# A decode step with grouped-query attention: the first softmax between two key halves, two small inputs as rows, the wait for the store in a section of its own

## The chip, the cores and the metric

The kernel runs on one core of one Trainium2 chip. The metric is the time of one execution on the device, in microseconds. A core has five engines that this kernel uses side by side: TensorE (PE: matrix products and transposes), VectorE (DVE), ScalarE (ACT), GpSimd (POOL, for a few fills at the start) and SyncE (SP, which here issues every transfer). Sixteen DMA engines carry the transfers. Engines run their own queues in order and wait for one another through semaphores.

## The reference, cut to what matters

One token `x` (512 values) goes through attention over a cache of 32,768 positions with 32 query heads on 8 key/value heads of width 128, and through a gated feed-forward layer; a gate computed from the token mixes the two.

```python
x = A_x                                             # (1, 1, 512)
g = sigmoid((x * gate_w).sum(-1, keepdims=True))
q = (x @ wq).reshape(B, Sq, 32, 128).transpose(0, 2, 1, 3)
k, v = repeat(k_cache, 4, axis=1), repeat(v_cache, 4, axis=1)   # caches: 1 x 8 x 32768 x 128
scores = einsum("bhqd,bhkd->bhqk", q, k) * 128 ** -0.5
o = einsum("bhqk,bhkd->bhqd", softmax(scores), v)
a = o.transpose(0, 2, 1, 3).reshape(B, Sq, 4096) @ wo
b = (silu(x @ w1) * (x @ w3)) @ w2                  # w1, w3: 512 x 1792
return g * a + (1 - g) * b
```

All is float32. The caches alone are 268 MB, and every byte is used once.

## The kernel before, in words

**Buffers.** Two large buffers in on-chip memory, `big_a` and `big_b`, have two halves of 4 MB each (32 KB on each of 128 partitions). Keys, values and the projection weights all pass through these halves.

**Start.** SP issues the two halves of `wq`, the token `x` and the gate weights between them, then `w1` and `w3` (L192 to L200). `x` and `gate_w` are laid out as 128 partitions by 4 values (`xs`, `gw`, L192 to L198). VectorE copies `xs` into the padded tile `xp` (L222), and TensorE multiplies `xp` with `wq` half by half (L250 to L261); the end of each half's products frees that half of `big_a` for keys. VectorE multiplies and adds `xs` and `gw` for the gate, TensorE sums over the partitions with a product with ones (L264 to L270). The feed-forward products follow (L290 to L309).

**The main loop.** The 8 key/value heads form four pairs, each pair is worked in four steps, and so there are 16 steps `t` (L444 to L463). A step has two halves of keys, `z` = 0 and 1, of 4 MB each. For one half, `scores` (L339) has VectorE turn the keys in 32 by 32 blocks, four instructions of 128 x 2048 into two buffers `kt` in turn, and TensorE multiply each quarter with a window of the queries (`winc`) that ScalarE copies ahead of the half (`window`, L325). After the two halves ScalarE copies the scores out (`scores_out`, L348) and TensorE clears its accumulator. `load_keys(t+1)` (L320) then puts the next step's two key loads into SP's queue. Each waits until TensorE has read the half that it overwrites. Keys go to `big_a`, only steps 1 and 3 go to `big_b`, before any values are there.

After every fourth step the pair's softmax is worked (`softmax(w)`, L364 to L397): TensorE turns the scores (four parts `f`, four transposes each), VectorE finds the maxima in 16 small and middling steps, subtracts them, ScalarE takes the exponentials, and VectorE sums these. In VectorE's queue all of it stands ahead of the next step's keys.

Values run some steps behind (`LAG` = 5, L142): from step 3 on, each step puts one 8 MB load of values into `big_b` (`load_values`, L400), behind the next step's two key loads. ScalarE copies the weights that belong to them (`weights`, L406), TensorE multiplies (`values_all`, L415), VectorE picks each head's own rows (`own`, L431).

**What sets the order.** The program lists the operations of all engines in one order by hand. A class `Program` (L24) records for each operation what it reads and writes, derives the semaphore waits and leaves out those that an earlier wait implies. Each engine's queue is then emitted in that order. Loads take one of 40 semaphores in turn (`load`, L182). TensorE's part of the main loop is a loop of its own on that engine (L658 to L673) that takes its permits from counting semaphores ("keys", "windows", "scores", "weights", "values"); its order is: values of an earlier step, windows and keys, clearing, and after each fourth step the four turning parts.

**End.** Output weights `wo` and the last values come through the same buffers, then `w2` (L554 to L634). VectorE copies the result out (L636), SP stores it (L637), waits for the store on SP (L643), and the section that holds the whole program (`tile_critical`, L151) closes when the function returns.

Of the kernel before, what the change touches and what calls it, by code (L numbers as in the profile page):

```python
# [9 lines left out]
ALU = mybir.AluOpType  # L10
AX = mybir.AxisListType
PE = mybir.EngineType.PE

P = 128
# [9 lines left out]
class Program:  # L24
# [16 lines left out]
            self.sems[name] = self.sem(name)  # L41
        return self.sems[name]

    def add(self, eng, fn, reads=(), writes=(), over=(), inc=None, by=1, credit=None, credits=(), loop=False):

        op = Op(eng, fn, credits, loop)
        clock = self.clock[eng]
        for c, _ in credits:
            for k, v in c.after.items():
                clock[k] = max(clock.get(k, 0), v)  # L50
        deps = {}
        for k in reads:
            assert k in self.writer, k
            deps[self.writer[k]] = True
        for k in (*writes, *over):
            if k in self.writer:
                deps[self.writer[k]] = True
            for r in self.readers.get(k, ()):
                deps.setdefault(r, False)
        need = {}  # L60
        taken = {c for c, _ in credits}
        for d, data in deps.items():
            if d in taken or (d.eng == eng and (eng == "PE" or not data)):
                continue
            if d.done is None:
                d = d.via
                if d is None or d.eng == eng:
                    assert d is not None
                    continue
            k, v = d.done  # L70
            if clock.get(k, 0) < v:
                need[k] = max(need.get(k, 0), v)
        for k, v in sorted(need.items(), key=lambda kv: -self.by[kv].index):
            if clock.get(k, 0) >= v:
                continue
            assert not loop, (fn, k, v)
            op.waits.append((k, v))
            for a, b in self.by[k, v].after.items():
                clock[a] = max(clock.get(a, 0), b)
        op.index = len(self.by)  # L80
        op.after = dict(clock)
        if credit:
            op.inc = (credit, by)
        elif inc is None and by == 0:
            op.inc = None
        else:
            s = inc or eng
            self.count[s] = self.count.get(s, 0) + by
            op.inc, op.done = (s, by), (s, self.count[s])
            op.after[s] = self.count[s]  # L90
            self.by[op.done] = op
        for c, _ in credits:
            c.via = op
        for k in reads:
            self.readers.setdefault(k, []).append(op)
        for k in writes:
            self.writer[k], self.readers[k] = op, []
        self.ops[eng].append(op)
        return op

# [14 lines left out]
def kernel(  # L115
# [32 lines left out]
    FJ = F // 4  # L148
    assert DH == P and D == 4 * P and REP == 4 and HKV == 8 and F == FR * P and S == 4 * P * NB

    ctx.enter_context(tc.tile_critical())  # L151
    pr = Program(nc, tc.alloc_semaphore)
    pe, dve, act, pool = (
        lambda fn, _e=e, **kw: pr.add(_e, fn, **kw) for e in ("PE", "DVE", "ACT", "POOL")
# [26 lines left out]

    def load(dst, src, writes, over=()):  # L182
        lanes[0] += 1
        return pr.add(
            "SP", lambda: nc.sync.dma_start(dst, src), writes=writes, over=over,  # L185
            inc=f"load{lanes[0] % 40}", by=16,
        )

    def region(b, z):
        return big[b][:, z * R:(z + 1) * R]  # L190

    xs, gw = sbuf("xs", NC), sbuf("gw", NC)  # L192
    wqd = wq.rearrange("(p c) n -> p (c n)", c=NC)
    for z in range(2):
        load(region(0, z), wqd[:, z * R:(z + 1) * R], [f"A{z}"])
        if z == 0:
            load(xs, x.rearrange("a b (p c) -> p (a b c)", p=P), ["xs"])
            load(gw, gate_w.rearrange("(p c) -> p c", p=P), ["gw"])  # L198
    for z, t in enumerate((w1, w3)):
        load(region(1, z)[:, 0:NC * F], t.rearrange("(p c) f -> p (c f)", c=NC), [f"B{z}"])  # L200

# [17 lines left out]
    dve(lambda: V.memset(xp, 0.0), writes=["xp0"])  # L219
    dve(lambda: V.memset(ones, 1.0), writes=["ones"])  # L220
    dve(lambda: V.memset(win, 0.0), writes=["win0"])
    dve(lambda: V.tensor_copy(xp[:, :, 0], xs), reads=["xs", "xp0"], writes=["xp"])  # L222

    for src, dst, view, axes in (
        ("ident", "fold", "p (c r) -> p r c", dict(c=4)),
# [21 lines left out]
    clear()  # L247


    for c in range(NC):  # L250
        def part(c=c):
            t = region(0, c // 2)
            for b in range(2):
                for j in range(4):
                    o = ((c % 2) * HKV + 4 * b + j) * REP * DH
                    ins = T.matmul(  # L256
                        pf[b][32 * j:32 * j + 32, :], xp[:, c, :], t[:, o:o + REP * DH],
                        start=(c == 0), stop=(c == NC - 1),
                    )
            return ins  # L260
        pe(part, reads=[f"A{c // 2}", "xp"], writes=["f0", "f1"])  # L261


    gpr, gsm = sbuf("gpr", NC), sbuf("gsm", 1)  # L264
    dve(lambda: V.tensor_mul(gpr, xs, gw), reads=["xs", "gw"], writes=["gpr"])
    dve(lambda: V.tensor_reduce(gsm, gpr, axis=AX.X, op=ALU.add), reads=["gpr"], writes=["gsm"])
    pe(lambda: T.matmul(pm[0][:, 0:1], ones, gsm, start=True, stop=True), reads=["ones", "gsm"], writes=["m0"])
    act(lambda: A.activation(gate[:, 0:1], pm[0][:, 0:1], AF.Sigmoid), reads=["m0"], writes=["gate0"])
    dve(lambda: V.tensor_scalar(gate[:, 1:2], gate[:, 0:1], -1.0, 1.0, op0=ALU.mult, op1=ALU.add),
        reads=["gate0"], writes=["gate1"])  # L270
# [87 lines left out]
    def turn_part(f):  # L358
        for a in range(4):
            ins = T.transpose(pf[f][:, P * a:P * a + P], sb[:, 4 * f + a].rearrange("p i m -> p (i m)"), ident)  # L360
        return ins

    def softmax(w):
        for f in range(4):  # L364
            pe(lambda f=f: turn_part(f), reads=[("sb", m) for m in range(4)] + ["ident"], writes=[f"f{f}"], loop=True)
            dve(lambda f=f: V.tensor_reduce(mx[:, f, :], pf[f].rearrange("p (n q) -> p q n", q=8), axis=AX.X, op=ALU.max),  # L366
                reads=[f"f{f}"], writes=[("mx", f)])

        dve(lambda: V.tensor_reduce(mt[:, 0:8], mx.rearrange("p f q -> p q f"), axis=AX.X, op=ALU.max),
            reads=[("mx", f) for f in range(4)], writes=["mt"])  # L370
        dve(lambda: V.transpose(mtt, mt), reads=["mt"], writes=["mtt"])
        for k in range(4):
            dve(lambda k=k: V.tensor_reduce(quads[0:32, k:k + 1], mtt[32 * k:32 * k + 32, :], axis=AX.X, op=ALU.max),  # L373
                reads=["mtt"], writes=[("quads", k)])
        dve(lambda: V.tensor_reduce(high[0:32, :], quads[0:32, :], axis=AX.X, op=ALU.max),
            reads=[("quads", k) for k in range(4)], writes=["high"])
        for k in range(4):
            dve(lambda k=k: V.tensor_copy(wide_t[32 * k:32 * k + 32, :], high[0:32, :].to_broadcast([32, 32])),  # L378
                reads=["high"], writes=[("wide_t", k)])
        dve(lambda: V.transpose(top, wide_t), reads=[("wide_t", k) for k in range(4)], writes=["top"])  # L380
        for f in range(4):
            d = rows[f % 2]
            dve(lambda f=f, d=d: V.tensor_tensor(  # L383
                d.rearrange("p (n q) -> p n q", q=8), pf[f].rearrange("p (n q) -> p n q", q=8),
                top[:, 0:8].unsqueeze(1).to_broadcast([P, 64, 8]), op=ALU.subtract,
            ), reads=[f"f{f}", "top"], writes=[f"row{f % 2}"])
            for u in range(2):
                act(lambda f=f, u=u, d=d: A.activation(  # L388
                    prob[u][:, 0:1024].rearrange("p (y n q) -> p n y q", y=16, q=4)[:, 4 * f:4 * f + 4],
                    d.rearrange("p (a y u q) -> p a y u q", a=4, y=16, u=2)[:, :, :, u],  # L390
                    AF.Exp, scale=SCALE,
                ), reads=[f"row{f % 2}"], writes=[("prob", u, f)])
        for u in range(2):
            dve(lambda u=u: V.tensor_reduce(  # L394
                sums[:, 8 * w + 4 * u:8 * w + 4 * u + 4], prob[u][:, 0:1024].rearrange("p (n q) -> p q n", q=4),
                axis=AX.X, op=ALU.add,
            ), reads=[("prob", u, f) for f in range(4)], writes=[("sums", w, u)])  # L397
# [46 lines left out]
    for t in range(NH):  # L444
        scores(t, 0, first)
        second = window(t, 1)
        if t >= LAG:
            own(t - LAG)
        if t >= LAG - 1:
            s = t - LAG + 1  # L450
            vals[s] = (vals[s], weights(s))
        scores(t, 1, second)
        scores_out(t)
        if t + 1 < NH:
            load_keys(t + 1)
        if t % 4 == 3:
            softmax(t // 4)
        if t + 1 < NH:
            first = window(t + 1, 0)
            if t >= LAG - 1:  # L460
                values_loop(*vals.pop(t - LAG + 1))
            if t >= LAG - 2:
                vals[t - LAG + 2] = load_values(t - LAG + 2)  # L463
# [176 lines left out]

    for e in ("SP", "ACT", "DVE", "POOL"):
        pr.emit(e)
    nc.sync.wait_ge(pr.semaphore("out"), 16)  # L643
    ops = pr.ops["PE"]
    a = next(i for i, o in enumerate(ops) if o.loop)
    b = max(i for i, o in enumerate(ops) if o.loop) + 1
# [11 lines left out]
    with nc.Fori(0, NP, 1, engines=[PE], head_slot={PE: 0}):  # L658
# [13 lines left out]
        for f in range(4):  # L672
            turn_part(f).then_inc(done, 1)  # L673
    pr.emit("PE", ops[b:])


# [26 lines left out]
```

## Time and profile before

| | us |
|---|---|
| median of 3 runs | 702.18 (701.09 to 702.6) |
| the profiled execution | 700.87 |
| its span in the profile | 699.1 |
| PE busy | 400.0 (57%) |
| DVE busy | 387.1 (55%) |
| ACT busy | 46.7 (7%) |
| key turning (L344, 128 instructions) | 285.9 of DVE's time |
| one key half, issue to landing, median | 28.1 |

The kernel moves 296.23 MB in the span, 424 GB/s. In the profile's views, an instruction's line is its line in the printed code; "idle before" is the time that the engine waited ahead of an instruction, with the engine or transfer that ended the wait. SPq is SP's queue: its entries are the issue of transfers, not the transfers. The DMA share of a stretch is the mean busy share of the 16 DMA engines; a packet is counted whole where the profile puts it, so the share of a short stretch can pass 1. PEclk is the share of TensorE's full clock that was granted.

### The profile page before, as it was taken

The numbers are of one execution on the slowest core, as the hardware profiler recorded it, in microseconds if no ns is written. First come the engines' busy times: TensorE is split into PE (matmuls) and PEld (weight loads), VectorE is DVE, ScalarE is ACT, GpSimd is POOL, SyncE is SP. The second block draws the span as 40 slices with busy tenths as digits, with TensorE's granted clock in tenths as the row PEclk, the third lists the DMA queues.
The fourth block names the chain that finished last, engine by engine and source line by source line (L and its number), as shares of the span: only waits on it lengthen the run. The fifth ranks groups of instructions, "written<-read, shape, count | busy, mean of one in ns | idle before, by whom it ended". The sixth has DMA issues, their size and how long they took to land. (4 is left out here: it accounts for less than half of the span.)

```text
span 699.1 us, 5711 instructions
## 1 busy us (share of the span) xinstructions
PE 400.0 (57%) x2384; PEld 91.3 (13%) x2384; DVE 387.1 (55%) x320; ACT 46.7 (7%) x106; POOL 1.5 (0%) x12
## 2 busy tenths in 40 slices
PE   3526665547565565757555655557466563835546
PEld 0100110101010111101010102101010102201112
DVE  1129998795709087754629097735538196532113
ACT  0100000110100002010100002000101002000000
POOL 0000000000000000000000000000000000000000
PEclk9976779769868878756677777868777886776669
DMA  8999999999999999999999999999999999999995
GB/s 360 433 435 433 435 426 437 452 396 409 452 412 439 427 457 411 433 433 441 446 407 437 431 454 409 439 426 452 420 427 439 424 457 406 423 448 420 419 417 235
DMA packets 10563, 296.37 MB, mean 424 GB/s; under 512 B 1332, under 2 KB 1336, under 8 KB 2488
## 3 DMA queue, kind: packets, MB, share of 16 engines
q1 hardware_dynamic: 10552, 296.23, 98.7%
q8 instruction: 6, 0.10, 0.1%
q14 instruction: 5, 0.04, 0.0%
HBM read 296.23 MB, written 0.00 MB: 424 GB/s over the span
## 5 line engine op out<-in xcount | busy, mean ns | idle before, releaser
L344 DVE STREAM_TRANSPOSE kt<-big_a 128x2048 f32<-128x2048 f32 x112 | 250.1, 2287 | 174.0 <-DMA big_a<-in_A_k_cache_dram 173.3
L333 PE MATMUL ps<-kt,winc 128*32 128x512 f32 x1024 | 191.4, 829 | 143.2 <-PEq L655 143.2
L421 PE MATMUL ps<-big_b,pv 128*32 128x512 f32 x768 | 109.2, 733 | 54.9 <-PEq L655 54.9
L333 PEld LDWEIGHTS ps<-kt,winc 128*32 128x32 f32 x1024 | 26.9, 124 | 303.1 <-issue 303.0
L421 PEld LDWEIGHTS ps<-big_b,pv 128*32 128x32 f32 x768 | 29.9, 131 | 132.8 <-issue 132.7
L344 DVE STREAM_TRANSPOSE kt<-big_b 128x2048 f32<-128x2048 f32 x16 | 35.8, 2288 | 3.3 <-DMA big_b<-in_A_k_cache_dram 3.0
L241 PE MATMUL ps<-acc 128*128 128x512 f32 x34 | 21.5, 718 | 21.8 <-PEq L655 20.2
L514 DVE SCALAR_TENSOR_TENSOR acc<-wo_t,own_rows,acc 128x512 f32<-128x512 f32 x24 | 18.0, 752 | 25.8 <-DMA wo_t<-in_A_wo_dram 25.0
L327 ACT COPY winc<-win 128x128 f32<-128x128 f32 x32 | 9.7, 303 | 330.0 <-PE ps L333 330.0
L530 PE MATMUL ps<-big_b,prob 128*32 128x512 f32 x128 | 18.9, 744 | 21.8 <-DMA big_b<-in_A_v_cache_dram 21.8
L350 ACT COPY sb<-ps 128x512 f32<-128x512 f32 x16 | 17.0, 1060 | 151.2 <-PE ps L333 151.2
L530 PE MATMUL ps<-big_a,prob 128*32 128x512 f32 x128 | 20.2, 797 | 5.3 <-DMA big_a<-in_A_v_cache_dram 5.3
L366 DVE TENSOR_REDUCE mx<-ps 128x8 f32<-128x512 f32 x16 | 9.9, 683 | 16.7 <-PE ps L360 16.7
L256 PE MATMUL ps<-big_a,xp 128*32 128x512 f32 x64 | 10.7, 827 | 14.8 <-DVE xp L222 10.0
L394 DVE TENSOR_REDUCE sums<-prob 128x4 f32<-128x1024 f32 x8 | 15.5, 1980 | 1.9 <-ACT prob L388 1.9
L296 PE MATMUL ps<-big_b,xp 128*32 128x448 f32 x64 | 7.8, 639 | 8.9 <-DMA big_b<-in_B_w_dram 8.9
L388 ACT ACTIVATE prob<-row 128x256 f32<-128x256 f32 x32 | 10.7, 404 | 29.3 <-DVE row L383 28.8
L503 PE MATMUL ps<-each,spot 128*128 128x64 f32 x6 | 2.1, 448 | 18.3 <-DVE each L500 18.3
L514 DVE SCALAR_TENSOR_TENSOR acc<-wo_t,on,acc 128x512 f32<-128x512 f32 x4 | 3.0, 752 | 16.4 <-DMA wo_t<-in_A_wo_dram 16.3
L437 DVE TENSOR_REDUCE red<-tmp 128x128 f32<-128x1024 f32 x6 | 11.5, 1915 | 0.2
L383 DVE TENSOR_TENSOR row<-ps,top 128x512 f32<-128x512 f32 x16 | 10.4, 689 | 0.9 <-ACT prob L388 0.8
L241 PEld LDWEIGHTS ps<-acc 128*128 128x128 f32 x34 | 5.7, 209 | 39.1 <-issue 37.5
(82 smaller groups left out, 100.1 us busy)
## 6 DMA issues: line engine op xcount, KB each, us to landing
big_a<-in_A_k_cache_dram SPq DMA_DIRECT2D x28, 4096.0 KB, 28.1
big_b<-in_A_k_cache_dram SPq DMA_DIRECT2D x4, 4096.0 KB, 31.4
big_a<-in_A_v_cache_dram SPq DMA_DIRECT2D x4, 4096.0 KB, 33.8
big_a<-in_A_wq_dram SPq DMA_DIRECT2D x2, 4096.0 KB, 16.7
wo_t<-in_A_wo_dram SPq DMA_DIRECT2D x4, 2048.0 KB, 18.1
big_b<-in_B_w_dram SPq DMA_DIRECT2D x2, 3584.0 KB, 33.6
big_b<-in_A_v_cache_dram SPq DMA_DIRECT2D x1, 4096.0 KB, 27.7
big_a<-in_B_w_dram SPq DMA_DIRECT2D x3, 1024.0 KB, 30.8
```

The source lines that it names most:

```text
L241: return T.matmul(ps_s, acc[:, 0:P], acc, start=True, stop=False, skip_group_check=True)
L256: ins = T.matmul(pf[b][32 * j:32 * j + 32, :], xp[:, c, :], t[:, o:o + REP * DH], start=(c == 0), stop=(c == NC - 1),)
L333: ins = T.matmul(ps_s[32 * g:32 * g + 32, :], winc[:, c, :], kt[c % 2][:, 512 * g:512 * g + 512], start=False, stop=False, skip_group_chec ...
L344: k = dve(lambda c=c, d=dst: V.transpose(d, kin[:, c]), reads=[key], writes=[f"kt{c % 2}"], credit="keys")
L350: lambda: A.copy(sb[:, :, :, t % 4], ps_s.rearrange("p (n i) -> p n i", i=32)),
L383: dve(lambda f=f, d=d: V.tensor_tensor(d.rearrange("p (n q) -> p n q", q=8), pf[f].rearrange("p (n q) -> p n q", q=8), top[:, 0:8].unsquee ...
L388: act(lambda f=f, u=u, d=d: A.activation(prob[u][:, 0:1024].rearrange("p (y n q) -> p n y q", y=16, q=4)[:, 4 * f:4 * f + 4], d.rearrange( ...
L394: dve(lambda u=u: V.tensor_reduce(sums[:, 8 * w + 4 * u:8 * w + 4 * u + 4], prob[u][:, 0:1024].rearrange("p (n q) -> p q n", q=4), axis=AX ...
L421: ins = T.matmul(ps_o[32 * t:32 * t + 32, :], pv[:, o:o + 32], big[1][:, n * P:(n + 4) * P], start=((z, g) == (0, 0)), stop=((z, g) == (1, ...
L437: dve(lambda: V.tensor_reduce(red[h], tmp.rearrange("p e b d -> p d (e b)"), axis=AX.X, op=ALU.add), reads=["tmp0", "tmp1"], writes=[("red ...
L514: dve(lambda k=k: V.scalar_tensor_tensor(acc, (wo_t if t is None else t)[:, k, :], o(k), acc, op0=ALU.mult, op1=ALU.add,), reads=[tkey, ke ...
L530: ins = T.matmul(ps_o[32 * t:32 * t + 32, :], prob[u][:, o:o + 32], vt[:, n * P:(n + 4) * P], start=((e, z, g) == (0, 0, 0)), stop=((e, z, ...
```

## The change

Four edits, in the order of the program:

1. Loads take one of 12 semaphores in turn instead of 40, and each load also depends on the load before it on the same semaphore (`lane`).
2. The token and the gate weights are loaded as one row of 512 values on one partition each, into the tiles `row0` and `row1`. TensorE turns the token's row into four columns (`columns`, four transposes) and VectorE copies these into `xp`, after its small set-up reductions. The gate's product and sum run over the 512 values on one partition, and the product with ones has one row.
3. TensorE's turning of the scores becomes a function of its own, `turn`, called where the softmax began. The rest of the first pair's softmax is called in step 4, after that step's first key half and ScalarE's copy for the second, ahead of the second half. The other pairs' softmaxes are called where they were, except that ScalarE's copy of the next window is listed ahead of them.
4. The section that holds the program closes before SP's wait for the store, and that wait stands in a second section of its own.

```diff
     def load(dst, src, writes, over=()):
         lanes[0] += 1
+        lane = f"load{lanes[0] % 12}"
         return pr.add(
-            "SP", lambda: nc.sync.dma_start(dst, src), writes=writes, over=over,
-            inc=f"load{lanes[0] % 40}", by=16,
+            "SP", lambda: nc.sync.dma_start(dst, src), writes=writes, over=[*over, lane], inc=lane, by=16, also=lane,
         )
...
         if z == 0:
-            load(xs, x.rearrange("a b (p c) -> p (a b c)", p=P), ["xs"])
-            load(gw, gate_w.rearrange("(p c) -> p c", p=P), ["gw"])
+            load(rows[0][0:1, :], x.rearrange("a b n -> (a b) n"), ["row0"])
+            load(rows[1][0:1, :], gate_w.rearrange("(o n) -> o n", o=1), ["row1"])
...
-    dve(lambda: V.tensor_copy(xp[:, :, 0], xs), reads=["xs", "xp0"], writes=["xp"])
...
+    def columns():
+        for c in range(NC):
+            ins = T.transpose(
+                pm[0][:, c:c + 1], rows[0][0:1, :].rearrange("o (p c) -> o c p", c=NC)[:, c, :], ident[0:1, 0:1]
+            )
+        return ins
+
+    pe(columns, reads=["row0", "ident"], writes=["m0"])
+    dve(lambda: V.tensor_copy(xp[:, :, 0], pm[0][:, 0:NC]), reads=["m0", "xp0"], writes=["xp"])
...
-    gpr, gsm = sbuf("gpr", NC), sbuf("gsm", 1)
-    dve(lambda: V.tensor_mul(gpr, xs, gw), reads=["xs", "gw"], writes=["gpr"])
-    dve(lambda: V.tensor_reduce(gsm, gpr, axis=AX.X, op=ALU.add), reads=["gpr"], writes=["gsm"])
-    pe(lambda: T.matmul(pm[0][:, 0:1], ones, gsm, start=True, stop=True), reads=["ones", "gsm"], writes=["m0"])
+    gpr, gsm = tmp[0:1, 1].rearrange("p b d -> p (b d)"), sbuf("gsm", 1)
+    dve(lambda: V.tensor_mul(gpr, rows[0][0:1, :], rows[1][0:1, :]), reads=["row0", "row1"], writes=["tmp1"])
+    dve(lambda: V.tensor_reduce(gsm[0:1, :], gpr, axis=AX.X, op=ALU.add), reads=["tmp1"], writes=["gsm"])
+    pe(lambda: T.matmul(pm[0][:, 0:1], ones[0:1, :], gsm[0:1, :], start=True, stop=True), reads=["ones", "gsm"], writes=["m0"])
...
+    def turn():
+        for f in range(4):
+            pe(lambda f=f: turn_part(f), reads=[("sb", m) for m in range(4)] + ["ident"], writes=[f"f{f}"], loop=True)
+
     def softmax(w):
         for f in range(4):
-            pe(lambda f=f: turn_part(f), reads=[("sb", m) for m in range(4)] + ["ident"], writes=[f"f{f}"], loop=True)
...
         scores(t, 0, first)
         second = window(t, 1)
+        if t == 4:
+            softmax(0)
         if t >= LAG:
             own(t - LAG)
...
         if t % 4 == 3:
+            turn()
+        if t + 1 < NH:
+            first = window(t + 1, 0)
+
+        if t in (7, 11, 15):
             softmax(t // 4)
         if t + 1 < NH:
-            first = window(t + 1, 0)
             if t >= LAG - 1:
...
-    nc.sync.wait_ge(pr.semaphore("out"), 16)
...
     pr.emit("PE", ops[b:])
+    critical.close()
+    with tc.tile_critical():
+        nc.sync.wait_ge(pr.semaphore("out"), 16)
```

In `Program.add`, `also` makes the operation the last writer of that name as well, and the first section is held in an `ExitStack` of its own so that it can be closed early.

More of the change, by code (lines that the diff above doesn't have):

```diff
@@ L42, in semaphore, with add @@
         return self.sems[name]
-    def add(self, eng, fn, reads=(), writes=(), over=(), inc=None, by=1, credit=None, credits=(), loop=False):
+    def add(self, eng, fn, reads=(), writes=(), over=(), inc=None, by=1, credit=None, credits=(), loop=False, also=None):
         op = Op(eng, fn, credits, loop)
@@ L97, in add @@
             self.writer[k], self.readers[k] = op, []
+        if also:
+            self.writer[also] = op
         self.ops[eng].append(op)
@@ L149 @@
     assert DH == P and D == 4 * P and REP == 4 and HKV == 8 and F == FR * P and S == 4 * P * NB
-    ctx.enter_context(tc.tile_critical())
+    critical = ctx.enter_context(ExitStack())
+    critical.enter_context(tc.tile_critical())
     pr = Program(nc, tc.alloc_semaphore)
@@ L190, in region @@
         return big[b][:, z * R:(z + 1) * R]
-    xs, gw = sbuf("xs", NC), sbuf("gw", NC)
     wqd = wq.rearrange("(p c) n -> p (c n)", c=NC)
```

## The prediction

> **What bounds the kernel.** I read the page's slices and DMA table first, then the stretches around the first softmax, then SP's and VectorE's instructions in order of time, and last the DMA packet records of the trace (start, length and bytes of each packet), transfer by transfer.
>
> ```profile
> DMA  8999999999999999999999999999999999999995
> q1 hardware_dynamic: 10552, 296.23, 98.7%
> ```
>
> SP's queue keeps the 16 DMA engines busy for 98.7% of the span, so only a hole in the DMA stream, or the two ends, can be worth anything. The packet records give the rate: a 32 KB packet takes 1.213 us, so a 4 MB transfer (eight packets on each engine) takes 9.71 us. From 208 to 586 us the last packets of the transfers come 9.68 to 9.72 us apart per 4 MB: no hole. One stretch breaks the pattern:
>
> ```profile
> core 0: us, PE busy (x) PEld busy (x) DVE busy (x) ACT busy (x) POOL busy (x), PEclk, DMA share, GB/s
> 140.00:150.00 10.00, 2.23 (x12) 0.46 (x16) 9.52 (x7) 1.66 (x6) 0.00 (x0) 0.50 0.98 426
> 150.00:160.00 10.00, 6.68 (x40) 0.79 (x32) 10.00 (x5) 0.82 (x2) 0.00 (x0) 0.82 0.90 370
> 160.00:170.00 10.00, 7.74 (x50) 1.82 (x54) 3.25 (x3) 1.16 (x2) 0.00 (x0) 0.83 0.94 400
> ```
>
> The DMA share falls to 0.90 while VectorE is busy for all of the 10 us. SP shows why (start, length of the group, line, count):
>
> ```profile
> 101.03 9.30 SPq L185 DMA_DIRECT2D big_a<-in_A_k_cache_dram  x2
> 130.22 0.33 SPq L404 DMA_DIRECT2D big_b<-in_A_v_cache_dram  x1
> 155.27 9.53 SPq L185 DMA_DIRECT2D big_a<-in_A_k_cache_dram  x2
> 173.84 0.33 SPq L404 DMA_DIRECT2D big_b<-in_A_v_cache_dram  x1
> ```
>
> I call the halves of step 5's keys k(5,0) and k(5,1), the value loads v(0), v(1). v(0) ends between 155.74 us (first engine) and 157.67 (last). k(5,0) is issued only at 155.27: it needs the buffer of k(4,0), which VectorE turns only after the first softmax:
>
> ```profile
> 119.46 8.95 DVE L344 STREAM_TRANSPOSE kt<-big_b 128x2048 f32<-128x2048 f32 x4 [1.14 <-DMA big_b<-in_A_k_cache_dram]
> 133.00 2.48 DVE L366 TENSOR_REDUCE mx<-ps 128x8 f32<-128x512 f32 x4 [4.58 <-PE ps L360]
> ...
> 145.06 17.73 DVE L344 STREAM_TRANSPOSE kt<-big_a 128x2048 f32<-128x2048 f32 x8
> ```
>
> VectorE waits 4.58 us for TensorE's transposes, then spends 133.00 to 145.06 on the softmax, while k(4,0), complete at 128.60, lies untouched. The first packet of k(5,0) starts 1.02 us after its issue, fifteen engines have begun by 157.68, the sixteenth begins at 158.81 (3.54 us after the issue). k(5,0) ends at 169.14, 11.47 us after v(0) instead of 9.71: **the hole costs the slowest engine 1.76 us**, and nothing later gives it back.
>
> **The change, part by part.**
>
> *1. The first softmax goes between the halves of step 4's keys.* Nothing is added; 12.06 us of VectorE work and the exps move behind four transposes. My rebuild, in the old run's times: k(4,0)'s last packet 128.60, plus the 0.57 us that k(3,1) took from its last packet (118.89) to the first transpose (119.46), gives 129.2. Two transposes of 2.24 (8.95/4) end at 133.6. The third overwrites a kt buffer that TensorE must have read; TensorE finishes its transposes at 134.3 and then takes 1.1 to 1.9 us for each of the four score groups (the clock granted decides). So the third starts at 135.4 to 136.2, the fourth ends at 139.8 to 140.7, and k(5,0) is issued at 141 to 142.7, over 12 us ahead of need: that hole is gone. Softmax: 140.3 + 12.06 = 152.3, four transposes to 161.3, TensorE's last group about 1.4 later: k(5,1) goes out near 162.7 (162.0 to 163.4; before, 164.47).
>
> What is late next is this k(5,1). Without the hole k(5,0) ends at 165.46 to 167.38. Fifteen engines get k(5,1) in time or are early ones with slack. The sixteenth would begin 3.5 to 4.2 us after the issue (k(5,0) and k(5,1) before), at 166.2 to 166.9, and a first packet after an idle engine is 0.35 to 0.65 longer: 177.2 at the end against 177.09 undisturbed; at the late end of the issue, 0.8 lost. I charge 0.25: **gain 1.5 us, bounds 0.8 and 1.76**. v(1) goes out some 9.4 us after k(5,1), as before, near 172.1, with k(5,1) ending at 175.2 or later: no new hole. SP issues in order and nothing overtakes. In the other pairs the window copy only moves ahead of the exps on ScalarE; VectorE's order and every release stay, and the queue there is 5.5 us or more ahead: nothing.
>
> *2. Token and gate weights as a row each.*
>
> ```profile
> xs<-in_A_x_dram SPq DMA_DIRECT2D x1, 2.0 KB, 11.9
> gw<-in_gate_w_dram SPq DMA_DIRECT2D x1, 2.0 KB, 12.0
> ```
>
> Each is 128 packets of 16 B now, 9 ns each: 16 data and 2 closing packets per engine, 0.16 us. The packets behind them are stretched by up to 0.37 us, and wq's second half ends at 22.34 to 23.30, where 9.71 after the first half's end (12.21 to 12.76) would be 21.92 to 22.47: lost 0.42 on the first engine, 0.83 on the last. A row is one piece of 2 KB; the closing store moves its four rows as one packet each, so I expect one packet on one engine, 88 ns as the 2,048-byte packets of wo take. Bounds of the gain: 0.83 if all goes, 0 if the stretching stays or falls on the slowest engine. I take **0.6**, nearer the upper end, as fifteen engines then have nothing to do.
>
> Added for it: four transposes on TensorE (0.27 us each, a pair every 0.2) and a copy of 0.17, some 1.0 us ahead of the first wq products (13.63 now). TensorE idles 4.74 us behind these before wq's second half lands, and the key load that they release (19.02) stands behind transfers that last until 40.9: hidden; uncovered it would cost 1.0. The gate's product and sum grow from 0.155 and 0.157 to about 0.69 and 0.68 (rows of 512 elements at L383 and L366), beside 14.36 us of VectorE waiting.
>
> *3. Twelve semaphores for loads.* A load also waits for the load twelve before it. At 28 us from issue to landing and 9.71 per load three or four are in flight; every wait is satisfied by the buffer's own: nothing.
>
> *4. The wait for the store in a section of its own.*
>
> ```profile
> L151 SPq NOP  x2: 17/18/18, 0.7 to 697.5; - x2
> L151 ACTq DRAIN  x1: 8/8/8, 697.2 to 697.2; - x1
> L698 SPq DRAIN  x3: 7/7/119, 697.6 to 698.4; - x3
> ```
>
> SP issues the store at 695.33 to 696.00 and passes its wait at 697.03. Only then do the section's closing steps run (L151, 697.19 to 697.52), then the program's (to 699.08). Now the first section closes beside the store's flight, and a second one, of SP alone, closes behind it. No engine has work queued behind. The gain is 0.33 if the second costs nothing; if it pays its own entry and close in full, 0.35 is lost. The clearing of semaphores (334 ns, on the chain) has 28 fewer to clear: 0 to 0.17. I take **0.25**, bounds 0.5 and -0.35.
>
> Sum: 1.5 + 0.6 + 0.25 = 2.35 us. The profiled execution took 700.87 us (span 699.1 and 1.77 around it), which becomes 698.5. The median shown, 702.18, lies 1.3 above it; the same saving there gives **699.8**.
>
> **A rule weighed.** The row first: a transfer that meets idle engines starts 1.02 us after its issue on the first and 3.54 on the last. The Trainium skill (DMA: Bandwidth & Descriptors, Specifications) gives a first-byte latency of about 0.6 us for loads issued from SP. By that, k(5,1) would start on every engine before it is due and part 1 would give 1.76. No packet of the trace began so soon after an issue, so the sum goes by the row.
>
> **The rivals.**
> - *A, the hole moves to k(5,1)* (chance 0.15). For: it is issued only 1.8 us earlier than before while its turn comes 1.76 us earlier. Against: 162.7 leaves the last engine about enough. If the issue stays at 164, part 1 gives 0.5: 702.18 - 0.5 - 0.85 = 700.8.
> - *B, slower: the softmax holds k(5,1) back* (0.07). It stands on VectorE ahead of the second half now; each us of issue past 163 costs one. The saving is eaten at 163 + 2.6 = 165.6. For: its exps bring a table load of 1.28 us, ScalarE's copy for the next window comes first, and TensorE's clock in this stretch was down to 0.50. Against: these lie beside 2.5 us of maxima and 2.5 us of small steps. At 167.5 it gives 702.18 + 1.9 = 704.1.
> - *C, only the softmax counts* (0.13): the rows stretch what follows as before and the second section costs 0.35: 702.18 - 1.5 + 0.35 = 701.0.
> - *D, every engine starts as early as the first did* (1.02 us after issue; 0.12), so k(5,1) loses nothing: 702.18 - 1.76 - 0.85 = 699.6. The Trainium skill's first-byte figure, above, points this way.
>
> The forecast has 0.53. **Chances**: the runs before differ by 1.5 us, so 0.2% (1.4 us) is about what a measurement of this kernel can tell from no change. Faster by more: forecast and D, 0.65; within: A and C, 0.28; slower: B, 0.07. **Range**: all bounds at their best save 1.76 + 0.83 + 0.5 = 3.1 (699.1), and the runs reach 1.1 below their median: 698.0. At the other end C and 1.3 for the spread of runs: 702.3. B and the tails are left out.
>
> **What would show it.** Right: keys of step 4 turned from 129 us, maxima after 139, k(5,0) issued at 141 to 143, k(5,1) at 162 to 163.5, the DMA share from 150 to 170 us near 1.0, packets under 512 B down from 1332 to about 1050, wq's second half landing 0.5 us or more sooner, L151's drains before the store's landing. Wrong: an issue of k(5,1) after 164, a last packet of step 5's keys less than 1 us before the old 178.89, or a chain behind the store longer than 2.05 us (697.03 to 699.08).

## The result and the profile after

| | before | changed |
|---|---|---|
| median of 5 runs | 701.15 us (701.07 to 702.6) | 698.40 us (698.34 to 698.44) |
| the profiled execution | 700.87 | 698.40 |
| its span | 699.1 | 696.5 |

The changed kernel takes 0.9954 of the time before (95% interval 0.994 to 0.9969): faster by 0.46%. Forecast were 699.8 us and 2.35 us saved; 698.4 us, and 2.75 us between these medians, came out. Where the runs before differ by 1.5 us, the five after lie within 0.1 us.

The page's DMA slices and table of the changed kernel, against a first slice of 8 and 98.7% before:

```profile
DMA  9999999999999999999999999999999999999995
DMA packets 10279, 296.37 MB, mean 426 GB/s; under 512 B 1046, under 2 KB 1050, under 8 KB 2204
q1 hardware_dynamic: 10268, 296.23, 98.9%
```

The bytes are the same, and 286 packets under 512 B are gone (1332 before): 256 of 16 B and 30 closing ones. SP's issues in order of time (start, length of the group):

```profile
100.41 10.38 SPq L189 DMA_DIRECT2D big_a<-in_A_k_cache_dram  x2
129.08 0.33 SPq L419 DMA_DIRECT2D big_b<-in_A_v_cache_dram  x1
139.98 22.02 SPq L189 DMA_DIRECT2D big_a<-in_A_k_cache_dram  x2
171.04 0.33 SPq L419 DMA_DIRECT2D big_b<-in_A_v_cache_dram  x1
```

k(5,0) goes out at 139.98 instead of 155.27. The group ends at 162.00 and one issue takes 0.33, so k(5,1) goes out at 161.67. This is a swap: one load goes out 15 us earlier, and the next, whose buffer now waits for the softmax, only 2.8 us earlier. VectorE in the same stretch:

```profile
118.86 8.96 DVE L356 STREAM_TRANSPOSE kt<-big_b 128x2048 f32<-128x2048 f32 x4 [0.51 <-DMA big_b<-in_A_k_cache_dram]
128.50 4.50 DVE L356 STREAM_TRANSPOSE kt<-big_a 128x2048 f32<-128x2048 f32 x2 [0.69 <-DMA big_a<-in_A_k_cache_dram]
134.21 4.50 DVE L356 STREAM_TRANSPOSE kt<-big_a 128x2048 f32<-128x2048 f32 x2 [1.21 <-PE ps L345]
138.64 2.44 DVE L381 TENSOR_REDUCE mx<-ps 128x8 f32<-128x512 f32 x4
...
150.68 8.94 DVE L356 STREAM_TRANSPOSE kt<-big_a 128x2048 f32<-128x2048 f32 x4
```

The wait of 4.58 us for TensorE's turning is now filled with two key transposes; 1.21 us of it is left ahead of the third. The softmax takes 12.04 us, 12.06 before.

In the packet records the last packet of k(5,0) comes 9.71 us after v(0)'s (11.47 before), that of k(5,1) 9.72 later: no hole. The 10-us shares show it less clearly:

```profile
150.00:160.00 10.00, 6.04 (x28) 0.92 (x32) 9.62 (x5) 0.00 (x0) 0.00 (x0) 0.50 0.95 410
160.00:170.00 10.00, 8.73 (x70) 2.20 (x66) 2.72 (x2) 1.17 (x2) 0.00 (x0) 0.93 1.01 433
```

The DMA shares (next to last column) are 0.95 and 1.01, where they were 0.90 and 0.94 before. Counted by the packets' own starts and lengths, the engines of the changed kernel are never idle from 150 to 170 us, and 0.95 us on average before. So 0.95 in a 10-us window is no hole here: 64 KB packets of 2.4 us fall to one window or the other.

The start and the end:

```profile
13.00 0.61 PE L253 MATMUL ps<-ident,row 1*128 1x1 f32 x4 [9.40 <-DMA row<-in_A_x_dram]
13.64 0.17 DVE L259 COPY xp<-ps 128x4 f32<-128x4 f32 x1 [10.01 <-PE ps L253]
13.72 0.67 DVE L277 TENSOR_TENSOR tmp<-row 1x512 f32<-1x512 f32 x1
```

```profile
L721 POOLq EVENT_SEMAPHORE_RANGE_CLEAR  x1: 182/182/182, 696.0 to 696.0; - x1
```

Four transposes and a copy put the first wq products at 13.86 (13.63 before). Each row moved as one packet of 2,048 B, 84 ns. wq's second half ends at 21.77 to 22.33, 0.97 us sooner on the last engine. From the store's issue to the end of the span 3.38 us pass (3.75 before); the clearing of semaphores fell from 334 to 182 ns.

### The profile page after: what moved, and what is told of

The parts are those of the page before. It is cut to its first block, busy times and chain, and to the rows that moved or that the text cites. A ratio compares the mean times of both kernels' runs of the same rounds, so it can differ in the third digit from the quotient of the medians.

```text
span 696.5 us, 5727 instructions
## 1 busy us (share of the span) xinstructions
PE 407.6 (59%) x2388; PEld 91.7 (13%) x2388; DVE 388.6 (56%) x320; ACT 46.5 (7%) x106; POOL 1.5 (0%) x12
## 5 line engine op out<-in xcount | busy, mean ns | idle before, releaser
L345 PE MATMUL ps<-kt,winc 128*32 128x512 f32 x1024 | 197.7, 854 | 134.4 <-PEq L675 134.3
L308 PE MATMUL ps<-big_b,xp 128*32 128x448 f32 x64 | 10.2, 803 | 9.5 <-DMA big_b<-in_B_w_dram 9.5
L268 PE MATMUL ps<-big_a,xp 128*32 128x512 f32 x64 | 9.3, 735 | 3.5 <-DMA big_a<-in_A_wq_dram 3.2
```

The source lines that it names most:

```text
L308: ins = T.matmul(pf[2 + z][32 * j:32 * j + 32, 0:FJ], xp[:, c, :], t[:, o:o + FJ], start=(c == 0), stop=(c == NC - 1),)
L345: ins = T.matmul(ps_s[32 * g:32 * g + 32, :], winc[:, c, :], kt[c % 2][:, 512 * g:512 * g + 512], start=False, stop=False, skip_group_chec ...
```

## The experiments

I went in with the theory of the prediction, now with the larger price: the hole behind v(0) is the main term, the start and the end are small. Rivals: the start and the end carry it, or the hole moves. The experiments were timed in three groups (e1 to e4, e5 to e8, e9 to e12), each on a chip of its own beside fresh runs of the kernel before.

### One part at a time

**e1**, the softmax moved and nothing else (`turn`, `softmax(0)` in step 4, the window copy ahead, on the kernel before; the copy's move was not tried alone):

```diff
+        if t == 4:
+            softmax(0)
...
         if t % 4 == 3:
+            turn()
+        if t + 1 < NH:
+            first = window(t + 1, 0)
+
+        if t in (7, 11, 15):
             softmax(t // 4)
         if t + 1 < NH:
-            first = window(t + 1, 0)
```

> The kernel before with the first softmax moved between the key halves of step 4, and nothing else. My theory (the hole behind v(0) cost the slowest DMA engine 1.76 us and nothing takes its place): 1.7 to 1.9 us less than before, k(5,0) issued near 140.6, k(5,1) near 162.3, the last packet of k(5,1) 19.4 us behind that of v(0). Rival 1 (the hole is only part; start and end made most of the 2.75 us): at most 1.2 us less. Rival 2 (the hole's cost varies from run to run and makes the spread of the runs before, 701.07 to 702.6): the runs of this kernel lie within 0.3 us of one another; if the spread has another source it stays near 1.5 us.

Measured: 699.10 us against 700.97 for the kernel before in this group, 1.87 less, ratio 0.9971 (0.9955 to 0.9986, or 1.0 to 3.2 us). Eleven of the twelve runs lie between 698.96 and 699.21, one at 700.3. SP's issues:

```profile
142.39 20.44 SPq L185 DMA_DIRECT2D big_a<-in_A_k_cache_dram  x2
171.88 0.33 SPq L407 DMA_DIRECT2D big_b<-in_A_v_cache_dram  x1
```

k(5,0) was issued at 142.39, k(5,1) at 162.51, and the last packet of k(5,1) came 19.42 us behind v(0)'s: no hole. The theory holds, and the runs are steady as rival 2 asked. Rival 1's 1.2 us is outside the median, though not clear of the interval; that the start and the end are small is shown by e5 to e8.

**e2**, the rows and nothing else (the diff's part 2 on the kernel before).

> The kernel before with token and gate weights as rows, and nothing else. My theory (the 256 packets of 16 B stretch what follows; rows are one packet each on one engine): wq's second half ends 0.6 to 1.0 us sooner, and 0.6 to 1.0 us off the whole. Rival (the hole behind v(0) takes it back, since k(5,0)'s issue follows the first softmax, and with it the landings, at the same distance): the hole moves along with the landings, so the gain stays; if instead the issue of k(5,0) were fixed by TensorE or VectorE the hole would grow by what the start gains and the whole would show nothing.

Measured: 700.84, ratio 0.9995 (0.9978 to 1.0012): nothing to be told from no change. wq's second half ended at 22.34 as in the changed kernel, 0.96 us sooner than before. The hole was there, with another price: k(5,0) took 11.79 us behind v(0) and k(5,1) 10.17, together 2.54 too much (1.81 before). k(5,0) went out 0.26 us ahead of the first engine's end of v(0), against 0.47 before: the landings came 0.48 us sooner and the issue only 0.28. That would fit the rival, which lets the hole grow by what the start gains; but e3, without the rows, stood at 0.24, so one execution of each does not decide it. The runs went from 699.71 to 702.41: against that spread 0.6 us could not be read.

**e3**, the wait for the store in a section of its own and nothing else.

> The kernel before with the wait for the store in a section of its own, and nothing else. My theory: of the 0.38 us that the stretch from the store's issue to the end of the span became shorter (3.75 to 3.37), 0.15 was the clearing of semaphores (334 to 182 ns, 28 fewer) and 0.23 the closing beside the store's flight; so here 0.2 to 0.25 less, the clearing still 334 ns. Rival (the second section costs as much as it hides, and all of the 0.38 came from the clearing and chance): 0 to 0.05 less.

Measured: 700.22, ratio 0.9986 (0.9971 to 1.0001), inconclusive by the time. One of the twelve runs took 1702.65 us, and its cause is not known. In the profile the stretch from the store's issue to the end was 3.55 us (3.75 before) with the clearing at 334 ns: 0.2, as expected of the section. This execution had the hole too: k(5,0) lost 1.34 us and k(5,1) another 0.70.

**e4**, the changed kernel with the first softmax back ahead of step 4's keys.

```diff
-        if t == 4:
-            softmax(0)
...
             turn()
+            softmax(t // 4)
```

> The changed kernel with the first softmax back ahead of step 4's keys. My theory (parts add): 0.9 to 1.3 us less than before and 1.6 to 1.8 more than the changed kernel; the hole is back with 11.3 to 11.6 us between the last packets of v(0) and k(5,0). Rival (without the late start the hole is smaller, parts overlap): less than 1.2 more than the changed kernel. If the hole makes the spread of the runs, the runs of this kernel spread over 0.5 us or more.

Measured: 699.75, ratio 0.9981 (0.9966 to 0.9996); 1.22 less than before, as expected, and 1.3 over the changed kernel's 698.4, which was timed apart from it. That lies between the theory's 1.6 to 1.8 and the rival's 1.2. Its runs spread from 698.49 to 700.82. In the profiled execution, the second fastest of the twelve (698.60), k(5,0) was issued at 154.24, 1.1 us ahead of the first engine's end of v(0), and the hole cost only 0.32 us there, 0.13 and 0.36 more at the next two transfers. My 11.3 to 11.6 us was wrong: 10.03. Where the hole is, its price is not one number; the fastest run of this kernel is within 0.1 of the changed kernel's.

### The small parts, read without the hole

With the softmax moved the runs are steady, so that a few tenths can be told.

**e5**: e1 and the rows. **e6**: e5 and the section, that is, all but the 12 semaphores. **e7**: the changed kernel once more. **e8**: the changed kernel with two loads of small packets put back, their tiles read by nobody:

```diff
+            load(sbuf("xs", NC), x.rearrange("a b (p c) -> p (a b c)", p=P), ["xs"])
+            load(sbuf("gw", NC), gate_w.rearrange("(p c) -> p c", p=P), ["gw"])
```

> The softmax moved and the rows, with the old end and 40 semaphores. Without the hole the runs lie within 0.1 to 0.2 us, so the small parts can be read here. My theory: the start gives 0.5 (the last packet in the profile came at 691.62 in the changed kernel and at 692.14 with the softmax alone), so 698.6 to 698.8. Rival (16 B packets cost the 0.83 us that wq's second half lost): 698.2 to 698.3.

> The changed kernel with 40 semaphores for loads instead of 12. My theory: the clearing of semaphores at the end is 334 ns again and the time 0.15 us over the changed kernel's, near 698.55; the second section itself is worth 0.2 against the same kernel with the old end (e5). Rival (the waits for the load twelve before, or their lack, do something in the loop): a difference away from 0.15 and other issue times of the loads.

> The changed kernel once more, as the anchor for the others of this group: 698.3 to 698.5, all runs within 0.2 us. If the steadiness was chance, the spread is over 0.5.

> The changed kernel with the two loads of 128 packets of 16 B put back behind the rows, their tiles read by nobody. My theory (the small packets alone cost what the rows save): wq's second half ends 0.8 to 1.0 us later than in the changed kernel, and the whole takes 0.4 to 0.7 more. Rival (it was the shape of the set-up work, VectorE's and TensorE's order at the start): within 0.1 of the changed kernel.

| kernel | median | runs | ratio to before (700.68) |
|---|---|---|---|
| e5 softmax, rows | 698.81 | 698.62 to 699.13 | 0.9969 (0.9958 to 0.9981) |
| e6 and section | 698.50 | 698.31 to 698.74 | 0.9966 (0.9955 to 0.9978) |
| e7 all | 698.48 | 698.31 to 698.62 | 0.9962 (0.9946 to 0.9978) |
| e8 all, small loads back | 698.79 | 698.50 to 699.06, one at 700.72 | 0.9970 (0.9959 to 0.9982) |

The small loads cost 0.31 us (e8 less e7): half of what I took for the rows, and less than the 0.4 to 0.7 expected of e8. From e1 to e5 the time falls by 0.29 too, but these ran on two chips, and the medians of the kernel before differ by the same 0.29 there (700.97 and 700.68), so this pair alone shows nothing. wq's second half in e8 ended at 23.50 us, 1.12 later than in e7; at the end of the loads only 0.17 of that is left (last packet 692.09 and 691.92). The section gives 0.31 in time (e5 less e6), of which the profiles show 0.20 behind the store's issue (3.76 and 3.56). The twelve semaphores give 0.02 in time, within the spread, though the clearing is 334 ns with 40 and 183 ns with 12:

```profile
L719 POOLq EVENT_SEMAPHORE_RANGE_CLEAR  x1: 334/334/334, 696.1 to 696.1; - x1
```

(e6; the changed kernel's line stands above.) k(5,1) went out at 161.43 in e6 and at 162.63 in e7. That is no sign of the semaphores: e5, which has 40, stands at 160.88, and the changed kernel's own first profile, which has 12, at 161.67. In SP's list of waits for the changed kernel no load waits for an earlier load.

### How late may k(5,1) be?

Dead maxima on VectorE behind the first softmax move k(5,1)'s issue and little else; 2, 4, 8 and 14 of them:

```diff
         if t == 4:
             softmax(0)
+            for _ in range(4):
+                dve(lambda: V.tensor_reduce(idle, pf[0].rearrange("p (n q) -> p q n", q=8), axis=AX.X, op=ALU.max),
+                    reads=["f0"], writes=["idle"])
```

> The changed kernel with 2 dead maxima (0.6 us each on VectorE) behind the first softmax, so that k(5,1) is issued 1.2 us later, near 163 to 164, 1 to 2 us ahead of the first engine's end of k(5,0) and 3 to 4 ahead of the last. The prediction's rule (the sixteenth engine starts 3.5 to 4.2 us after the issue and pays a longer first packet): 0.5 to 1.5 us over the changed kernel. Rival D (engines start 1.0 to 1.9 us after the issue): within 0.2 of it.

> The same with 4 maxima: k(5,1) issued near 164.5 to 165.5, at the first engine's end of k(5,0) and 2 ahead of the last, as k(5,0) stood to v(0) in the kernel before. Both theories: a hole of that kind is back, 0.5 to 2 us over the changed kernel, and the runs spread over 0.5 us or more where the changed kernel's lie within 0.3.

> The same with 8 maxima: k(5,1) issued near 167 to 168, behind the last engine's end of k(5,0). Start on the first engines 1.0 us after the issue, on most 1.9: the last packet 2.5 to 3.5 us later than in the changed kernel, the whole 2.5 to 4 more: slower than the kernel before, which is rival B of the prediction at work.

> The same with 14 maxima: k(5,1) issued near 170.5 to 171.5, 4 us behind the last engine's end. From here each us of VectorE costs one: 6 to 7.5 us over the changed kernel (3.6 more than with 8 maxima). Rival (the values and weights behind it hide part): less than 2.5 more than with 8.

The kernel before took 700.83 in this group. One such maximum takes 0.69 us. The lead is from a load's issue to the first engine's end of the transfer in front; the cost is what the distance between last packets has over 9.71 us per 4 MB (19.35 for values).

| kernel | median (runs) | k(5,1): issue, lead, cost | v(1): lead, cost |
|---|---|---|---|
| e9, 2 maxima | 698.66 (698.35 to 700.70) | 162.89, 2.17, 0.01 | 2.50, 0 |
| e10, 4 | 700.26 (698.71 to 702.94) | 164.54, 0.52, 0.16 | 1.80, 1.82 |
| e11, 8 | 703.04 (701.75 to 704.29) | 167.97, -2.90, 3.08 | 1.80, 2.13 |
| e12, 14 | 706.98 (706.74 to 708.09) | 171.53, -6.41, 6.92 | 1.73, 1.84 |

The shares of e11, in the columns of the prediction's table, show what a real hole looks like there, in the stretch 160 to 170:

```profile
160.00:170.00 10.00, 6.35 (x34) 1.14 (x34) 9.25 (x6) 1.19 (x2) 0.00 (x0) 0.83 0.68 272
```

and SP's issues of e10 how little it takes (k(5,1) out at 140.08 + 24.79 - 0.33):

```profile
140.08 24.79 SPq L189 DMA_DIRECT2D big_a<-in_A_k_cache_dram  x2
173.91 0.33 SPq L419 DMA_DIRECT2D big_b<-in_A_v_cache_dram  x1
```

e9 keeps the time in six of its eleven runs (698.35 to 698.66) and takes 0.7 to 2.2 us more than e7's 698.48 in the other five; its profile is of one of the six. So two maxima are enough to bring a hole back in some executions: the changed kernel stands that close to it. e10 costs 1.8 over the 698.48 of e7 and is as spread as the kernel before. e11 is slower than the kernel before, 1.0034 (1.0021 to 1.0047), and e12 more, 1.0093 (1.0078 to 1.0108): this is rival B at its work. Both cost more than I expected: 4.6 over e7 against 2.5 to 4, and 8.5 against 6 to 7.5, since the value load behind k(5,1) lost about 2 us as well. A straight line from e10 to e11 crosses the time before at an issue of 165.2; the prediction's break-even was 165.6. That they are so near is partly luck, as the prediction had no loss at v(1). From e11 to e12 an issue 3.56 us later costs 3.94.

## Why the prediction was right or wrong

- **What bounds the kernel, and the hole: right.** After the change the DMA engines ran without a hole from 13 us until the first of them had finished its loads at 688.8 us, and e1 alone brought 1.87 us.
- **The rebuilt order: right.** Keys of step 4 from 128.5 (129 forecast), maxima at 138.6 (139.8 to 140.7), k(5,0) at 139.98 (141 to 142.7), k(5,1) at 161.67 (162 to 163.4), v(1) at 171.04 (172.1). The forecasts are in the old run's times, and the rows had moved v(0)'s last packet 0.6 us ahead; in e1, without the rows, k(5,0) at 142.39 and k(5,1) at 162.51 lie inside the forecast.
- **The charge of 0.25 for k(5,1): wrong.** "The sixteenth would begin 3.5 to 4.2 us after the issue" was read where engines were running dry, and such starts came back there: in e10 to e12, at leads of 1.73 to 1.80 us, the last engine began v(1) 3.66, 3.99 and 3.89 us after the issue, and the load lost 1.8 to 2.1 us. At leads of 2.17 us and more behind a stream without a hole (e1, e5, e7, e9 and the changed kernel) no engine idled and nothing was lost. In e11, where all engines had run dry, their first packets started 0.96 to 1.91 us after the issue; in e11 and e12 the last engine's last packet came 11.75 and 11.85 us after the issue, 2.0 to 2.1 over eight packets. Rival D, which the Trainium skill's 0.6 us (DMA: Bandwidth & Descriptors, Specifications) pointed to, came nearer in the time, but no run here bears out a start of every engine within 0.6 or 1.02 us.
- **The hole at 1.5: too small**, 1.87 measured, though 1.5 lies within the interval of 1.0 to 3.2; by the packets the hole cost 1.81 and k(5,1) nothing after the change. More than the charge was off: I took its price from one execution. At k(5,0) it was 1.76 there, 2.08 in e2, 1.34 in e3 and 0.32 in e4 (1.81, 2.54, 2.04 and 0.81 with the transfers right behind). "Nothing later gives it back" does not hold everywhere either: e4's last packet of step 6's first keys came 0.84 us later than e7's (206.43 and 205.59), and at the end of the loads both stood at 691.93. And the runs of kernels that have it spread over 2 to 5 us (699.49 to 704.52 before, but for one run far outside), while those without lie within 0.1 to 0.6 us, single runs aside. Why the price changes from one execution to the next stays open: with a lead of 1.8 us, k(5,1) lost 0.70 in e3 and v(1) 1.82 in e10.
- **The step that failed is the last one: "The median shown, 702.18, lies 1.3 above it; the same saving there gives 699.8."** It carries the 1.3 us over as if it lay outside the change. The 702.18 was the median of three runs of a kernel that spreads over 4 to 5 us; 35, 26 and 23 runs of it beside the experiments have medians of 700.97, 700.68 and 700.83, so the profiled execution's 700.87 was the better base. The spread belongs to the hole and goes with it: eleven of e1's twelve runs lie within 0.25 us, and after the change median and profiled execution are both 698.40. The same sum against the profiled execution, "which becomes 698.5", met it within 0.1. That is partly luck: 0.37 too little for the hole and 0.3 too much for the rows cancel. The saving of 2.75 against the five-run median is 0.4 above the 2.35 of the sum; beside e7 it was 2.20 (700.68 to 698.48). The medians of 5 to 35 runs of the kernel before differ by half a microsecond from group to group.
- **The rows at 0.6: twice too much**, 0.3 measured by putting the small loads back (e8). The mechanism held (one packet each, wq 0.97 us sooner). What the early engines gained was not on the path: the last packet of w3 came at 40.56, only 0.36 sooner (40.92). In the records a 16 KB packet of the instruction queue at 35.87 us stands right ahead of a packet stretched by 0.55, and such stretches of 0.4 to 0.7 recur (47, 112, 192, 375, 583, 598, 614, 663 us); the first engine ends its loads some 2.8 us before the last. That these few engines set the end, whatever the others gain, is argued from the records and was not tried.
- **The end at 0.25: right in size**, 0.31 to 0.33 in time (e5 to e6 and e7). By the profile 0.2 is the section (e3, and e5 to e6), and the clearing is 0.15 shorter. The first section's drains stand at 693.9 us, ahead of the store's landing, as forecast. The second section is not free: SP reaches its wait for the store at 695.20 us, when the store's last packet has been there since 694.49.
- **Edits costed at nothing: right.** The rows' extra work moved wq's products by 0.23 us (1.0 was the price if uncovered), ahead of 3.2 us of idle time, and the gate's row work took 2 x 0.67 us beside VectorE's wait.

## What to carry to other kernels

When a transfer queue never stops, look for the one place where it does, and compare the time of a load's issue with the end of the transfer ahead of it: in the profiled executions here a lead of 2.1 us or more cost at most 0.13 us, and leads of 0.2 to 1.8 us cost 0.16 to 2.13. Moving long work out of one load's way puts it into the next load's way, so rebuild both issue times before trusting the gain. A hole has no fixed price: take it from the spread of many runs, and do not carry one run's offset past the change that removes its cause.

## What was not expected of the hardware

- A load that goes out while only some engines are running dry can reach its last engine later (up to 4.2 us after the issue before, 3.7 to 4.0 in e10 to e12) than one that finds all of them dry (1.91 in e11).
- A queue that runs dry costs more than the idle time. The first packets after it took up to 0.92 us longer than 1.213 (before; the prediction read 0.35 to 0.65); in e3, where k(5,1) had a lead of 1.81 us, single packets took up to 2.92 us.
- The steadiness: 0.1 us over the five runs of the first result without the hole, where kernels with it vary by 2 to 5 us at the same bytes.
- A share of 0.94 or 0.95 in a 10-us window stood for no idle time at all (e1 and the changed kernel), so such shares are to be checked against the packets.
